# Attention with routed experts on one core: shorter blanks behind each expert's tokens, spaced scatters of one group, ranking of the experts ahead of the head's outputs

## The chip, the cores and the metric

One core of one Trainium2 chip runs the kernel. The metric is the device time of an execution in microseconds (us). Three executions of the kernel before took 619.24 to 621.92 us, with a median of 619.53 us.

## The reference

Attention over 8 batches, 8 heads, 576 positions and 64 features, with a causal window of 128 and a linear bias by distance; the heads side by side give 4608 tokens of 512 features. Each token then goes to one of 8 experts, and the expert's output is scaled by the probability of the choice.

```python
rel = pos[:, None] - pos[None, :]
scores = np.where((rel >= 0) & (rel < 128), q @ k.T / 8 - slope[h] * np.abs(rel), -1e9)
x = (softmax(scores) @ v)                     # then (8 * 576, 8 * 64)
logits = (x / |x|) @ (emb / |emb|).T / tau
expert_idx = np.argmax(logits, axis=1)
probs = softmax(logits)
for e in range(8):
    mask = expert_idx == e
    h = np.maximum(x[mask] @ w1[e], 0.0)      # 512 -> 1024
    out[mask] = gate_w[mask, None] * (h @ w2[e])   # 1024 -> 512
```

With the inputs used, the eight experts receive 611, 541, 517, 513, 507, 670, 573 and 676 tokens.

## The kernel before, in words

Attention works on 36 tiles of 128 tokens, each in two halves. All of it is cut into jobs with an engine, an estimated length, predecessors and a due time; the class `Plan` runs through them once on the host and so fixes the order of instructions on every engine. A job marked `fill` runs where an engine would be free otherwise. A predecessor can carry an extra delay in ns, which moves only the plan's times; `ORDER` (-1e9) in that place asks for order alone. On the chip, engines wait on semaphores for the data and never on the planned times.

Finished tiles are normalised (L718, L724), split into two f16 halves in `rows_buf` (L737 on ACT, L750 on POOL), transposed by a DMA (L754) and multiplied with the expert embeddings on PE (L762, tile `board`). Tiles are routed in groups, `GROUPS = [8, 8, 8, 6, 4, 2]`: a chain of small instructions on DVE and PE finds each token's expert and its place among the expert's tokens, and `put` then scatters a tile's 128 rows to the expert's rows in the DRAM tensor `xs` (L862, indirect DMA on POOL; 36 in all, named `put0` to `put35`). If two puts are neighbours on POOL, a small memset (L861) stands between them. Group 3 holds tiles 24 to 29. In the plan, the puts of groups 0 to 2 have due times 6.4 us apart, those of later groups 1.2 us.

After three groups the fullest expert so far is known, and its first 384 rows, the "head", are computed inside attention as filling work on PE (L937 to L961): `head_y` scales the outputs (L968 on ACT, L970 on DVE) and `head_put` writes them out (L973, L395, POOL). After the last group, DVE ranks the experts by their counts (L378 to L388, eleven small instructions), which gives `ebi` and `nki`, the number of the s-th expert and its count.

The second part, `moe`, goes over the experts by rank in the order `TURNS = [0, 1, 4, 3, 5, 6, 2, 7]`; rank s is computed at a fixed size `SLOTS = [672, 688, 624, 576, 544, 528, 528, 512]`, whatever its count (for rank 0 without the 384 rows of the head). A second plan orders these jobs. For each expert SyncE (SP) does in turn: `blank_rows` (L1251 to L1264), which writes zero rows from the tile `zrow` behind the expert's tokens, so that rows past the count hold no garbage; `rows` (L1266), which reads the expert's rows transposed into `xT` (L1273) and their token numbers and weights (`info`, L1278 and L1285); and `fetch` (L1319, L1321), which loads the weights in f32 into a ring of five buffers `ws`. ACT and DVE split the weights into f16 halves (`w1h` and `w2h`, L1339 and L1347; `w1l` and `w2l`, L1337 and L1350). PE multiplies: `hidden` (L1506), or `product` by a scheme with fewer products (L1455, whose results `e` on ACT and `u` on DVE combine), and `output` (L1555). L1568 and L1570 scale, and POOL scatters to the output (L395). The reading of `rows` waits until the blank and all scatters have landed; a blank need not wait for scatters, which write other rows.

The blank before is one DMA per expert of a fixed number of rows: 288 for rank 0 and 704, 640, 576, 544, 544, 544 and 512 for ranks 1 to 7, of 514 words each. It starts at the expert's count, so it always reaches past the slot's end.

Of the kernel before, what the change touches and what calls it, by code (L numbers as in the profile page):

```python
# [23 lines left out]
P = 128  # L24
# [8 lines left out]
ROW = 514  # L33
SLOTS = [672, 688, 624, 576, 544, 528, 528, 512]
# [14 lines left out]
ORDER = -1e9  # L49
# [12 lines left out]
EXPERT = 9000  # L62
DUE = {'av': -80.7, 'exp': -3.6, 'flip': -24.6, 'gap': 6.4, 'k': -18.2, 'load': -6.9, 'loadv': -2.3, 'logit': -8.2, 'mask': 6.9, 'max': 2.6, 'merge': 1.6, 'norm': 10.8, 'phi': -14.6, 'place': 36.6, 'plo': 1.7, 'put': 18.0, 'q': -14.3, 'route': -1.9, 'score': -29.7, 'v': 3.1, 'xdma': 9.2, 'xhi': 13.9, 'xlo': 16.9, 'xnorm': 24.9}
LAST = 3
MASK = [1230, 1650]
PUT_LANDS, HEAD_LANDS = 4200, 2400

# [98 lines left out]
def kernel(  # L166
# [11 lines left out]
    nc = tc.nc  # L178
# [40 lines left out]
    xs = dram.tile([E, SEG, ROW], F32, name="xs")  # L219
# [33 lines left out]
    zrow = const.tile([P, ROW], F32, name="zrow")  # L253
# [63 lines left out]
    scatters = []  # L317
# [84 lines left out]
    def attention(actx):  # L402
# [6 lines left out]
        stg = actx.enter_context(tc.tile_pool(name="stg", bufs=STG))  # L409
# [555 lines left out]
        def head_y(a):  # L965
            hd["y", a] = y = stg.tile([P, DM], F32, tag="stg", name=f"y_head_{a}")
            if a % 2:
                nc.scalar.activation(y, hd["ps2", a], AF.Copy, scale=hd["gs"][:, a : a + 1])  # L968
            else:
                nc.vector.tensor_scalar(y, hd["ps2", a], hd["gs"][:, a : a + 1], None, op0=ALU.mult)  # L970
# [6 lines left out]
        J = plan.job  # L977
# [155 lines left out]
        def of(gi, what, i):  # L1133
            def f():
                if gi not in box:
                    box[gi] = route_ops(gi)
                x = box[gi][what]
                return x(i) if what == 3 else x() if what == 4 else x[i][2]()

            return f  # L1140

        for gi, G in enumerate(groups):
            T0 = sum(groups[:gi])
            u = 2 * (T0 + G) - 1
            tail = gi == len(groups) - 1
            kinds = [[(e, ns) for e, ns, _ in of_kinds(gi)[w]] for w in (1, 2, 6)]
            prev = [f"xnorm{T}" for T in range(T0, T0 + G)]
            for i, (e, ns) in enumerate(kinds[2]):
                J(f"norm{gi}_{i}", e, ns, of(gi, 5, i), after=prev, due=due("route", u) + 150 * i, uses=[("gn", gi)])
                prev = [f"norm{gi}_{i}"]  # L1150
            scaled = prev[0]
            prev = [f"logit{T0 + G - 1}", "expert_rows", "tables"]
            for i, (e, ns) in enumerate(kinds[0]):
                J(
                    f"route{gi}_{i}", e, ns, of(gi, 1, i), after=prev + ([f"total{gi - 1}"] if i == R_RANK and gi else []), due=due("route", u) + 150 * i,
                    makes=[("rkb", ("rkb", gi))] if i == R_RANK else [], uses=[("rkb", gi)] * (i >= R_RANK),
                )
                prev = [f"route{gi}_{i}"]
                if i == R_RANK - 1:
                    J(f"total{gi}", "DVE", 0 if tail else 270, of(gi, 4, 0), after=prev, due=due("route", u) + 5000)  # L1160
            done = prev[0]
            prev = [f"route{gi}_2", scaled]
            rows_ = [("gx", T) for T in range(T0, T0 + G)]
            for i, (e, ns) in enumerate(kinds[1]):
                J(f"gate{gi}_{i}", e, ns, of(gi, 2, i), after=prev, due=due("route", u) + 150 * (i + 8), uses=rows_ if i in (0, 5) else [])
                prev = [f"gate{gi}_{i}"] if i else prev
            if tail:
                before = [f"route{gi}_{R_RANK}"]
                for i in range(4):
                    J(f"count{i}", "DVE", 90, lambda i=i: count_ops(box[gi][0])[i][2](), after=before, due=due("route", u) + 150 * (i + 10))  # L1170
                    before = [f"count{i}"]
                for i, (e, ns, f) in enumerate(rank_ops({})):
                    J(f"order{i}", e, ns, f, after=before, due=due("route", u) + 150 * (i + 30))
                    before = [f"order{i}"]
            for g in range(G):
                J(
                    f"put{T0 + g}", "POOL", 1180 if gi < LAST else 1270, of(gi, 3, g), dma=750, after=[done, prev[0], f"gate{gi}_0", f"xlo{T0 + g}"], uses=[("gx", T0 + g)],
                    due=due("put", u) + (1000 * DUE["gap"] if gi < LAST else 1200) * g,
                )
            if gi == GP:  # L1180
                ops = [(e, ns) for e, ns, _ in head_ops({})][1:]
                prev = [f"route{gi}_{R_RANK + 1}", "expert_rows"]
                for i, (e, ns) in enumerate(ops):
                    J(f"head{i}", e, ns, (lambda i=i: head_ops(box[GP][0])[1 + i][2]()), after=prev, due=due("route", u) + 150 * (i + 18))
                    prev = [f"head{i}"]
                started = prev[0]
# [21 lines left out]
        for a in range(HEAD // P):  # L1208
            for c in range(6):
                dep = [f"hlo{ft}" for ft in range(FT)] + [f"wlo{2 * KT + i}" for i in range(FT)] if c == 0 else [f"out{a}_{c - 1}"]  # L1210
                J(
                    f"out{a}_{c}", "PE", 4 * 216, lambda b=(a, c): head_output(*b), after=dep + ([f"out{a - 1}_5"] if a and c == 0 else []),
                    makes=[(RING["sc"], ("ps2", a))] if c == 0 else [], uses=[("ps2", a)], due=2e7 + 1000 * a, fill=True,
                )
            J(f"y{a}", "ACT" if a % 2 else "DVE", 600, lambda a=a: head_y(a), after=[f"out{a}_5", "head_info"] + [f"fetch{i}" for i in range(NP)], makes=[("stg", ("y", a))], uses=[("ps2", a)], due=2e7)
            J(f"yput{a}", "POOL", 1200, lambda a=a: head_put(a), after=[f"y{a}"], uses=[("y", a)], due=3e7)
        handed["free"], end = plan.run(dict(FREE))
        handed["rows"] = max(end[f"put{T}"] for T in range(NT)) + LAT["SP"]
# [8 lines left out]
    def moe(mctx):  # L1227
# [25 lines left out]
        def blank_rows(s):  # L1253
            (nb, hb), b0 = blocks(s), first_row(s) // P
            e = state[s]["e"]
            nt = sel_["n0i"][0:1, 0:1] if s == 0 else nki[0:1, s : s + 1]
            n = nc.sync.value_load(nt, min_val=0, max_val=NTOK)
            m = (nb - b0) * P + hb
            d = nc.sync.dma_start(
                xs[ds(e, 1), ds(n, m), :].rearrange("o (a p) c -> p (o a) c", p=32),  # L1260
                zrow[0:32].unsqueeze(1).to_broadcast([32, m // 32, ROW]),
            )
            for p_ in scatters:
                tc.declare_no_dep(d.ins, p_.ins, reason="rows beyond the expert's tokens")  # L1264

        def rows(s):  # L1266
            cap, r0, (nb, hb) = SLOTS[s], first_row(s), blocks(s)
# [688 lines left out]
```

## Time and profile before

| | before |
|---|---|
| median of 3 runs | 619.53 us |
| the profiled execution | 615.1 us |
| its span, first to last instruction | 612.9 us |
| mean granted TensorE clock | 0.974 |
| PE busy | 565.2 us (92%) |
| DVE busy | 476.7 us (78%) |
| ACT busy | 372.0 us (61%) |
| POOL busy | 330.0 us (54%) |

All times in the text are from the profiled execution, counted in us from the start of its span; 2.2 us of that execution lie outside the span. A granted clock of 1.00 is 2.4 GHz on PE and 0.50 is 1.2 GHz. Attention fills the span to about 254 us, where the head's last output ends; the experts follow.

### The profile page before, as it was taken

How to read it: one execution, taken by the hardware profiler on the slowest of the kernel's cores; microseconds unless marked ns; L12 is line 12 of the kernel's file. 1: busy time of each engine (PE TensorE's matmuls, PEld its weight loads, DVE VectorE, ACT ScalarE, POOL GpSimd, SP SyncE). 2: the span in 40 equal slices, each digit the busy share in tenths (PEclk: the TensorE clock that was granted, in tenths of full speed). 3: DMA queues.
4: the chain of work that ended last, by engine and by line, in shares of the span. 5: the costliest groups of instructions: out<-in, count | busy, mean ns of one | idle time of the engine just before them, and what ended most of it. 6: DMA issues, size and time to landing. Idle time of an engine off the chain costs nothing. (4 is left out here: it accounts for less than half of the span.)

```text
span 612.9 us, 16467 instructions
## 1 busy us (share of the span) xinstructions
PE 565.2 (92%) x6097; PEld 369.5 (60%) x6097; DVE 476.7 (78%) x1573; ACT 372.0 (61%) x858; POOL 330.0 (54%) x435
## 2 busy tenths in 40 slices
PE   7999889799978699798999899999899999999996
PEld 3767667666656466363654574574674854754854
DVE  5988988989989676235598796699699799898570
ACT  4999999999999682134462443653653645734320
POOL 7888699899889865302355711442515334433001
PEclk9999999999988989888999999999999999999999
DMA  8699979999999944899978437528658354412001
GB/s 262 162 226 228 242 197 193 255 211 237 232 278 254 200 118 107 213 234 298 269 183 229 190 106 177 185 70 183 249 136 235 127 155 156 136 64 87 14 18 53
DMA packets 121298, 109.88 MB, mean 179 GB/s; under 512 B 85109, under 2 KB 86133, under 8 KB 121216
## 3 DMA queue, kind: packets, MB, share of 16 engines
q1 hardware_dynamic: 115376, 89.89, 59.7%
q0 software_dynamic: 5840, 18.92, 8.2%
q8 instruction: 49, 0.80, 0.5%
q14 instruction: 33, 0.27, 0.1%
HBM read 61.92 MB, written 28.12 MB: 147 GB/s over the span
## 5 line engine op out<-in xcount | busy, mean ns | idle before, releaser
L395 POOL DMA_INDIRECT out_dram<-y,ids x32 | 42.8, 1338 | 132.3 <-ACT y L1568 100.2
L599 ACT ACTIVATE pe<-sb,nm 128x128 f32<-128x128 f32 x288 | 94.8, 390 | 12.2 <-DVE nm L591 11.9
L1555 PE MATMUL ps<-w2h,hh 128*128 128x512 f16 (+1 forms) x264 | 98.4, 373 | 0.0
L1555 PE MATMUL ps<-w2l,hh 128*128 128x512 f16 (+1 forms) x264 | 98.4, 373 | 0.0
L1555 PE MATMUL ps<-w2h,hl 128*128 128x512 f16 (+1 forms) x264 | 98.4, 373 | 0.0
L1555 PEld LDWEIGHTS <-hh 128*128 128x128 f16 x528 | 51.5, 98 | 58.0 <-issue 0.8
L608 PE MATMUL ptp<-ident,pe 128*128 128x128 f32 x288 | 57.8, 302 | 16.5 <-ACT pe L599 6.0
L564 PE MATMUL sc<-k,q 64*64 64x192 f32 (+1 forms) x1152 | 62.4, 333 | 0.0
L512 ACT ACTIVATE pq<-ptp 128x512 f16<-128x512 f32 x78 | 57.5, 737 | 7.7 <-PE ptp L608 6.4
L1568 ACT ACTIVATE y<-ps,gs 128x512 f32<-128x512 f32 (+1 forms) x28 | 19.0, 678 | 70.0 <-PE ps L1555 56.3
L515 DVE SCALAR_TENSOR_TENSOR pq<-ptp,pq 128x512 f16<-128x512 f32 x66 | 49.1, 744 | 9.4 <-ACT pq L512 7.7
L591 DVE CUSTOM_DVE_ANT_0 sb<-sc,tab_full 128x128 f32<-128x128 f32 x224 | 54.7, 279 | 0.0
L608 PEld LDWEIGHTS ptp<-ident,pe 128*128 128x128 f32 x288 | 34.0, 144 | 33.0 <-ACT pe L599 17.9
L1506 PE MATMUL ps<-xT,w1h 128*128 128x288 f16 (+2 forms) x192 | 43.7, 322 | 5.7 <-DMA xT<-xs 3.9
L750 POOL TENSOR_TENSOR rows_buf<-xf,rows_buf 128x512 f16<-128x512 f32 x36 | 43.9, 1221 | 5.3 <-ACT rows_buf L737 5.0
L1337 DVE SCALAR_TENSOR_TENSOR w2l<-ws,w2h 128x1024 f16<-128x1024 f32 x28 | 33.6, 1219 | 16.1 <-ACT w2h L1339 16.1
L1350 DVE SCALAR_TENSOR_TENSOR w1l<-ws,w1h 128x512 f16<-128x512 f32 (+1 forms) x36 | 37.5, 1050 | 9.2 <-ACT w1h L1347 9.2
L1455 PEld LDWEIGHTS <-w1h 128*128 128x128 f16 x384 | 37.6, 98 | 11.6 <-issue 2.7
L564 PEld LDWEIGHTS sc<-k,q 64*64 64x64 f32 x1152 | 37.3, 137 | 11.3 <-issue 5.2
L1555 PEld LDWEIGHTS <-hl 128*128 128x128 f16 x264 | 25.8, 98 | 29.5
L862 POOL DMA_INDIRECT xs<-rows_buf,di x36 | 36.1, 1003 | 12.5 <-issue 4.1
L694 PE MATMUL av<-vh,mp 128*128 128x65 f16 x384 | 39.2, 196 | 3.5 <-POOL mp L646 3.3
(257 smaller groups left out, 1661.2 us busy)
## 6 DMA issues: line engine op xcount, KB each, us to landing
ws<-moe_w_dram SPq DMA_DIRECT2D x56, 512.0 KB
q<-q_dram SPq DMA_DIRECT2D x36, 256.0 KB
ldv<-v_dram SPq DMA_DIRECT2D x36, 256.0 KB
k<-k_dram SPq DMA_DIRECT2D x32, 256.0 KB
stg<-moe_w_dram SPq DMA_DIRECT2D x16, 256.0 KB
xs<-zrow SPq DMA_DIRECT2D x3, 1092.2 KB
xs<-zrow SPq DMA_DIRECT2D x1, 1413.5 KB
xs<-zrow SPq DMA_DIRECT2D x1, 1285.0 KB
```

The costliest lines, as they stand in the source:

```text
L395: ins = nc.gpsimd.indirect_dma_start(out[:, :], bass.IndirectOffsetOnAxis(ap=ids, axis=0), y, None, bounds_check=NTOK - 1, oob_is_err=False)
L512: nc.scalar.activation(hi, ps, AF.Copy, scale=scale)
L515: nc.vector.scalar_tensor_tensor(lo, ps, scale, hi, op0=ALU.mult, op1=ALU.subtract)
L564: nc.tensor.matmul(sc[T, hf, j][l * REM : (l + 1) * REM, i, c0 : c0 + (n1 - n0) * REM].rearrange("p (n c) -> p n c", c=REM), qT[T][rows, h ...
L591: nc.vector.tensor_tensor_reduce(sb_t[T, hf][:, 2 * j + i, :], sc[T, hf, j][:, i, c0 : c0 + P], tab, -QS, BIG, ALU.add, ALU.min, nm_t[T, h ...
L599: nc.scalar.activation(pr_t[T, hf][:, n, :], sb_t[T, hf][:, n, :], AF.Exp, bias=nm_t[T, hf][:, n : n + 1], scale=-1.0)
L608: nc.tensor.matmul(pt.rearrange("p (l j) c -> p l j c", j=2)[:, :, j, i * REM : (i + 1) * REM], pe[:, n, :], ident.rearrange("p (l c) -> p ...
L694: nc.tensor.matmul(o_, a_, b_, start=False, stop=(n == last), skip_group_check=True)
L750: nc.gpsimd.tensor_tensor(xx[:, DM : 2 * DM], xf_t[T], xx[:, 0:DM], op=ALU.subtract)
L1455: nc.tensor.matmul(pq[key], a, b, start=(first and i == 0), stop=(i == len(jobs) - 1), skip_group_check=True)
L1506: nc.tensor.matmul(ps[:, :w], a[:, kt, fs], xx[:, b + kt, c0 : c0 + w], start=(n == 0), stop=(n == len(jobs) - 1))
L1555: nc.tensor.matmul(ps, x[:, ft, a * P : (a + 1) * P], w[:, ft, c], start=(which != 2 and n == 0), stop=(which != 1 and n == len(jobs) - 1) ...
```

## The change

Three edits. First, `blank_rows` issues two DMAs: one of 128 rows, and one for the rest of the old length with a condition, `n + 128 < SLOTS[s]`, n being the expert's count read into a register (for rank 0 its count past the head). With the counts above, n + 128 is at least the slot's size for every rank: 670 + 128 against 672 is the first, 507 + 128 against 512 the last. Second, each scatter of group 3 but its first gets the scatter before it as a predecessor with an extra 2600 ns. Third, the head's `y` jobs come after the last job of the ranking (`order10`) in order.

```diff
 LAST = 3
+SPREAD = 2600
...
                 J(
-                    f"put{T0 + g}", "POOL", 1180 if gi < LAST else 1270, of(gi, 3, g), dma=750, after=[done, prev[0], f"gate{gi}_0", f"xlo{T0 + g}"], uses=[("gx", T0 + g)],
+                    f"put{T0 + g}", "POOL", 1180 if gi < LAST else 1270, of(gi, 3, g), dma=750, after=[done, prev[0], f"gate{gi}_0", f"xlo{T0 + g}"] + ([(f"put{T0 + g - 1}", SPREAD)] if gi == LAST and g else []), uses=[("gx", T0 + g)],
...
-            J(f"y{a}", "ACT" if a % 2 else "DVE", 600, lambda a=a: head_y(a), after=[f"out{a}_5", "head_info"] + [f"fetch{i}" for i in range(NP)], makes=[("stg", ("y", a))], uses=[("ps2", a)], due=2e7)
+            J(f"y{a}", "ACT" if a % 2 else "DVE", 600, lambda a=a: head_y(a), after=[f"out{a}_5", "head_info", ("order10", ORDER)] + [f"fetch{i}" for i in range(NP)], makes=[("stg", ("y", a))], uses=[("ps2", a)], due=2e7)
...
             m = (nb - b0) * P + hb
-            d = nc.sync.dma_start(
-                xs[ds(e, 1), ds(n, m), :].rearrange("o (a p) c -> p (o a) c", p=32),
-                zrow[0:32].unsqueeze(1).to_broadcast([32, m // 32, ROW]),
+            dl = [nc.sync.dma_start(xs[ds(e, 1), ds(n, P), :].rearrange("o p c -> (o p) c"), zrow)]
+            dl.append(
+                nc.sync.dma_start(
+                    xs[ds(e, 1), ds(n + P, m - P), :].rearrange("o (a p) c -> p (o a) c", p=32),
+                    zrow[0:32].unsqueeze(1).to_broadcast([32, (m - P) // 32, ROW]),
+                    cond=(n + P < SLOTS[s]), cond_hint=False,
+                )
             )
-            for p_ in scatters:
-                tc.declare_no_dep(d.ins, p_.ins, reason="rows beyond the expert's tokens")
+            for d in dl:
+                for p_ in scatters:
+                    tc.declare_no_dep(d.ins, p_.ins, reason="rows beyond the expert's tokens")
```

The new lines shift the numbers: L862 is L863 afterwards, L1259 becomes L1260 and L1262, L1273 becomes L1279.

On POOL, around group 3's scatters, the order before (the L646 rows are the masks of attention, which PE waits for; L750 is the low half of a tile):

```order
L646 AFFINE_SELECT mp_33_1_5553<-pq_33_1_5495 128x512
L862 DMA xs_66<-rows_buf_200,di_3_5565 42496x514
L861 MEMSET spare_201 128x1
L862 DMA xs_66<-rows_buf_200,di_3_5565 42496x514
L861 MEMSET spare_201 128x1
...
L862 DMA xs_66<-rows_buf_200,di_3_5565 42496x514
L646 AFFINE_SELECT md_34_0_5763<-pq_34_0_5585 128x512
L646 AFFINE_SELECT mp_34_0_5762<-pq_34_0_5585 128x512
```

and with the change:

```order
L647 AFFINE_SELECT mp_33_1_5553<-pq_33_1_5495 128x512
L863 DMA xs_66<-rows_buf_200,di_3_5565 42496x514
L647 AFFINE_SELECT md_34_0_5637<-pq_34_0_5585 128x512
L647 AFFINE_SELECT mp_34_0_5636<-pq_34_0_5585 128x512
L751 TENSOR_TENSOR rows_buf_200<-xf_32_5443,rows_buf_200 128x512
L863 DMA xs_66<-rows_buf_200,di_3_5565 42496x514
L535 TENSOR_TENSOR vo_35_5756<-ldv_35_5375,vh_193 128x512
L647 AFFINE_SELECT md_34_1_5782<-pq_34_1_5666 128x512
...
L863 DMA xs_66<-rows_buf_200,di_3_5565 42496x514
L862 MEMSET spare_201 128x1
L863 DMA xs_66<-rows_buf_200,di_3_5565 42496x514
L751 TENSOR_TENSOR rows_buf_200<-xf_35_5946,rows_buf_200 128x512
```

Six scatters in a row become four that have three to five other instructions behind each of them, and a pair at the end, ahead of the last tile's low half. The six scatters of groups 4 and 5 stay in one row.

On SP, the blank of the second expert (rank 1) with what each instruction waits for, before (in brackets stand the semaphores, of which DMAHW0 to 7 count landings of SP's DMAs in turn):

```order
L1257 TENSOR_LOAD nki [waits DVE_49]
L1257 ISA x2
L1259 ISA
L1259 DMA xs<-zrow 32x22x514 [waits DMAHW4_49,DMAHW5_49,DMAHW3_49,DMAHW2_49]
L1321 ISA
L1321 DMA ws_1_0_6438<-moe_w_dram 128x2x512 [waits DMAHW6_49]
```

and with the change:

```order
L1258 TENSOR_LOAD nki [waits DVE_49]
L1258 ISA x2
L1260 ISA
L1260 DMA xs<-zrow 128x514 [waits DMAHW5_49,DMAHW6_49,DMAHW4_49,DMAHW3_49]
L1262 ISA x2
L1262 DMA xs<-zrow 32x18x514 [waits DMAHW7_49,DMAHW6_49]
L1327 ISA
L1327 DMA ws_1_0_6436<-moe_w_dram 128x2x512
```

The conditional DMA waits for two landings, DMAHW6 being that of the 128 rows just issued; the weights stand behind it on SP. Each of the eight blanks has this form.

On DVE, the ranking before (its eleven instructions in order, the first two ahead of the head's output):

```order
L378 SCALAR_TENSOR_TENSOR key<-cnt,desc_e 128x8
L379 SCALAR_TENSOR_TENSOR key<-ho,key 128x8
L970 TENSOR_SCALAR y_head_6235<-ps_head_6148,gs_head 128x512
L380 TENSOR_TENSOR gtm<-key 128x64
L375 TENSOR_REDUCE rank<-gtm 128x8
```

and with the change:

```order
L379 SCALAR_TENSOR_TENSOR key<-cnt,desc_e 128x8
L380 SCALAR_TENSOR_TENSOR key<-ho,key 128x8
L381 TENSOR_TENSOR gtm<-key 128x64
...
L389 CAST nki<-nk 128x8
L971 TENSOR_SCALAR y_head_6258<-ps_head_6141,gs_head 128x512
```

All eleven now stand ahead of it. The rest of DVE's, PE's and ACT's order in `moe` is the same, but for a few head jobs and scalings that changed places with a neighbour.

## Rows read from the trace of the kernel before

**Rows 1.** PE's waits by line and releaser, 250 to 612 us (total, times, longest)
```profile
PE ps L1506 <- DMA xT<-xs: 3.9, 1, 3.9
PE pq_b L1455 <- DVE u L1473: 2.0, 1, 2.0
PE ps L1506 <- ACT w1h L1339: 1.9, 1, 1.9
PE pq_a L1455 <- ACT e L1466: 1.6, 1, 1.6
PE ps L1506 <- DVE w1l L1337: 0.8, 1, 0.8
```
**Rows 2.** Windows: us, busy us (instructions) of PE, PEld, DVE, ACT, POOL, then granted clock, DMA share, GB/s
```profile
212.90:219.70 6.80, 4.61 (x26) 2.35 (x26) 3.23 (x16) 4.08 (x12) 2.54 (x5) 0.50 0.60 158
225.00:240.00 15.00, 15.00 (x187) 10.09 (x185) 12.50 (x41) 6.77 (x17) 8.75 (x13) 1.00 0.48 84
257.30:264.10 6.80, 5.71 (x24) 3.52 (x25) 1.68 (x2) 0.83 (x2) 0.79 (x4) 0.50 0.74 168
288.00:291.40 3.40, 3.40 (x12) 1.79 (x13) 1.66 (x2) 1.14 (x2) 0.79 (x1) 0.50 1.06 301
349.50:352.90 3.40, 3.40 (x17) 2.27 (x15) 3.40 (x4) 1.26 (x2) 3.40 (x7) 0.50 0.27 108
```
**Rows 3.** POOL's timeline, 205 to 240 us (start, us, instruction, idle before and its releaser)
```profile
207.06 1.02 POOL L862 DMA_INDIRECT xs<-rows_buf,di  x1 [0.16 <-POOL mp L646]
...
213.43 0.96 POOL L862 DMA_INDIRECT xs<-rows_buf,di  x1 [0.19 <-issue]
214.41 0.65 POOL L646 TENSOR_SCALAR_AFFINE_SELECT md<-pq 128x512 f32<-128x512 f32 x1
...
235.01 1.16 POOL L750 TENSOR_TENSOR rows_buf<-xf,rows_buf 128x512 f16<-128x512 f32 x1 [2.71 <-ACT rows_buf L737]
```
**Rows 4.** PE's timeline, 207 to 217 us
```profile
210.77 0.43 PE L762 MATMUL board<-enc,xT 128*128 128x8 f16 x11 [1.04 <-DMA xT<-rows_buf]
...
212.85 0.33 PE L608 MATMUL ptp<-ident,pe 128*128 128x128 f32 x1 [1.09 <-issue]
215.38 0.77 PE L608 MATMUL ptp<-ident,pe 128*128 128x128 f32 x2 [2.19 <-issue]
```
**Rows 5.** DVE's timeline, 247 to 251 us: the head's first output, the ranking behind it
```profile
248.17 0.75 DVE L970 TENSOR_SCALAR y_head<-ps_head,gs_head 128x512 f32<-128x512 f32 x1 [3.77 <-remote]
...
250.25 0.17 DVE L388 CAST nki<-nk 128x8 int32<-128x8 f32 x1
```
**Rows 6.** SP's timeline, 244 to 330 us (issues: start, us)
```profile
245.27 0.13 SPq L1259 DMA_DIRECT2D xs<-zrow  x1
...
252.86 3.45 SPq L1273 DMA_TRANSPOSE xT<-xs  x1
...
259.50 0.36 SPq L1259 DMA_DIRECT2D xs<-zrow  x1
...
260.66 2.17 SPq L1319 DMA_DIRECT2D ws<-moe_w_dram  x1
268.97 6.36 SPq L1273 DMA_TRANSPOSE xT<-xs  x1
...
324.46 0.38 SPq L1259 DMA_DIRECT2D xs<-zrow  x1
```
**Rows 7.** SP's waits, 244 to 612 us (columns as in rows 1)
```profile
SPq L1273 <- DMA xs<-rows_buf,di: 0.3, 1, 0.3
```
**Rows 8.** Windows while the second expert's blank moves, and just after it (columns as above)
```profile
260.40:267.70 7.30, 7.30 (x47) 5.10 (x46) 1.37 (x3) 1.64 (x4) 0.00 (x0) 0.74 0.96 198
267.80:271.00 3.20, 3.20 (x29) 2.56 (x27) 0.82 (x2) 0.77 (x2) 0.00 (x0) 1.00 0.99 330
```
**Rows 9.** ACT's timeline near 334 us
```profile
333.61 1.06 ACT L1339 ACTIVATE w2h<-ws 128x1024 f16<-128x1024 f32 x1 [6.33 <-DMA ws<-moe_w_dram]
```
**Rows 10.** Window around PE's wait for `u` (columns as above)
```profile
345.00:360.00 15.00, 12.83 (x94) 9.80 (x93) 15.00 (x28) 6.77 (x17) 7.74 (x10) 0.89 0.26 88
```

## The prediction

> **What bounds the kernel now.** PE is busy 92% of the span, so what counts is where it isn't. I read PE's waits first [rows 1]: behind attention PE waits 3.9 us for the first expert's rows at the handoff, 1.9 and 0.8 us for weights of the second expert (ACT's `w1h`, DVE's `w1l`), 2.0 us for DVE's `u` and 1.6 us for ACT's `e`. Then the windows in which the granted clock was half [rows 2]: each comes right behind a stretch in which PE sat idle. 6.8 us at 0.50 lie around 213 to 220 and 257 to 264 us, 3.4 us behind 288 and 349.5 us. A stretch at half the clock with PE busy gives back half of its length when it goes: 1.7 us for one of 3.4. So a wait on PE costs more than itself, and less of it can give back more.
>
> Inside attention I then read 205 to 217 us. POOL issues six scatters in a row from 207.06, the last at 213.43 us [rows 3], about 1.27 us apart, and only then the masks that attention needs, at 214.41. In the same stretch PE is idle for 1.04, 1.09 and 2.19 us [rows 4]; the last two are called issue, waits for nothing that the profile shows, and end right behind the scatters. From 225 to 240 us PE is busy 15.00 of 15 us [rows 2], so time won ahead of that is passed on.
>
> **Scatters of group 3.** With three to five other instructions behind each of the first four scatters, masks come ahead of the second scatter and not behind the sixth. At most all idle time goes: 1.04 + 1.09 + 2.19 = 4.3 us, and the half clock, under which PE was busy 4.61 us [rows 2], gives back 2.3: 6.6 us. At least nothing goes, if the scatters stall PE wherever they stand. The 1.04 us ends with a transposing DMA, which the change does not touch; I leave it. Of the other 3.28 + 2.3 = 5.6 us I leave a fifth to the pair of scatters that still stands together: **-4.5 us** (0 to -6.6). The pair now stands ahead of the last tile's `L750`, ahead of which POOL had 2.71 us idle [rows 3]: two scatters at 1.27 us are 2.5 us and just fit. If they don't, the last group's routing is late, and with it the handoff.
>
> **Ranking and the first blank.** Before, DVE's first head output waited 3.77 us until 248.17 with the ranking behind it, which ended at 250.42 [rows 5]. Now the instructions behind it (1.5 us by those rows) run in that gap, from 244.40, and end near 246. SP needs `ebi` for the weights ahead of the first rows, which it issued at 252.86 [rows 6], after a wait for the last scatter of only 0.3 us [rows 7]: ranking, blank and scatters ended almost together, so all must move. The ranking moves by some 4 us. The blank issued at 245.27 shrinks from 288 to 128 rows of 2056 bytes, 329 kB less; at 198 GB/s [rows 8] that is 1.66 us, by which the scatters' packets behind it come earlier. Against that SP now waits for the 128 rows to land, which I work out below as 3.5 us: 248.8, with the ranking done and before the scatters end. The handoff shrinks by **-1.6 us** (0 to -1.6 of idle; up to -3.3 if the half clock behind it shortens by one step of 3.4 us too, which I don't count, since an idle 2.19 us went with a 6.8 us stretch).
>
> **The second blank.** It was issued at 259.50 and the rows behind it at 268.97 [rows 6]: 9.47 us. Of these 7.3 us moved 704 x 2056 = 1447 kB at 198 GB/s with the DMA engines 0.96 busy [rows 8]; 2.17 us are start and landing. 128 rows are 263 kB: 1.33 + 2.17 = 3.5 us. The conditional DMA is not sent, but SP stands at it until 263.0. Behind it stand two weight loads; before, they were issued by 262.83 (260.66 + 2.17) [rows 6], within 3.0 us after the blank's 0.36. If they take 3.0 us again, rows go out at 266.0, 3.0 us earlier, and so does every load behind them. That covers the 1.85 + 0.79 = 2.64 us on `w1h` and `w1l` [rows 1], and with the idle time the half clock behind it goes: **-4.3 us** (0, if another load is late by as much, to -4.3). Late next would be DVE's `w1l`, with 0.4 us to spare.
>
> The Trainium skill speaks against this edit: "DMA: Bandwidth & Descriptors", section "Rules for kernel authors", advises joining small transfers into one large one, and its section "Anatomy of one DMA — SWDGE (gpsimd) path" fits a DMA as 2.0 us plus bytes over 436 GB/s. By that fit the old blank is an estimated 5.3 us and 128 rows 2.6 us, so the 2.6 us for which SP is now held would eat the 2.7 us won: this term about 0 and the sum -7. The 9.47 us of this trace disagree; the measurement decides.
>
> **The blank at 324.46** [rows 6] moved 544 rows; 416 fewer are 4.3 us at 198 GB/s, less about 2.2 us for the landing that the loads behind it now wait for: 2.1 us. ACT's `w2h` at 333.61 had waited 6.33 us for a load [rows 9], and two steps on stands PE's wait of 2.0 us for `u`. But DVE is then busy 15.00 of 15 us [rows 10], so part of that is its own work. I take half the wait and leave the clock: **-1.0 us** (0 to -2.0 - 1.7 = -3.7).
>
> **The other five blanks**, and 16 more SP instructions: 0. No wait in rows 1 ends with what stands behind them; the 1.6 us on `e` is ACT's own. If that cover is gone, each can cost up to the 2.2 us of a landing.
>
> **Sum:** -4.5 - 1.6 - 4.3 - 1.0 = -11.4 us. Against the profiled 615.1 us that is 603.7; the median of the runs shown is 4.4 us higher, 619.53, which gives **608 us**.
>
> **Rivals.**
> 1. *The scatters stall PE wherever they stand*, or the stall passes to the pair and the six behind it. For it: groups 4 and 5 keep their row of six, and PE's late signals had no releaser that I can name. Against it: POOL's masks stand behind the burst. Only the blanks gain: -6.9, 612.6 us.
> 2. *The blanks' bytes were hidden.* Weights and DVE set the pace behind the handoff: for it, DVE's 15.00 of 15 [rows 10]; against it, PE waits for what loads feed [rows 1, 9]. Left are -4.5 and -1.6: 613.4 us.
> 3. *The condition does not spare the bytes.* The second DMA runs for all rows, or its wait lasts as long. Then each blank takes its old time and a landing more: the handoff and both weight waits grow by about 2.2 us at two places, the scatters still gain 4.5: about 619 us. Against it: n + 128 reaches the slot's size for all eight counts.
> 4. *SP's hold costs more than the bytes* (slower). Loads are issued 3.0 us later at the second blank and at that of 324.46, and the first blank is held 3.5 us for 1.66 us of bytes: +1.8 + 3.0 + 3.0 = +7.8 if PE waits for loads by their issue and not by bytes, less 4.5: +3.3, 622.8 us. It decides where DMA engines had room beside the blank, so that a load issued early also landed early. Against it: 0.96 busy at 198 GB/s, and 330 GB/s only after it [rows 8]. The same page of the Trainium skill, section "Rules for kernel authors", advises to issue a DMA early and wait on its semaphore late; here SP does the opposite, and no trace of before shows what that costs.
> 5. *Everything goes in full:* -6.6 - 3.3 - 4.3 - 3.7 = -17.9, 601.6 us.
>
> **How the numbers follow.** About 0.5%, 3.1 us, is what a measurement of this kernel can tell from no change, so faster is below 616.4. Forecast 0.47; rival 1 0.17; 2 0.16; 3 0.08; 4 0.06; 5 0.06. The forecast, 5 and nearly all of 1 and 2 are faster: 0.82. Rival 3 and the weak ends of 1 and 2 are the same: 0.13; slower 0.05. The range takes in the forecast with its terms' bounds, 1, 2 and most of 5: 602 to 616; the outer ends of 3 and 4 are left out.
>
> **What would show it.** In the profile after: masks between the scatters, and no `issue` wait of 1 us or more on PE near 213 to 216; no 6.8 us at half the clock there. DVE's ranking before its first head output. Blank DMAs of 257 KB (eight, and no others), 3.5 us from issue to the load behind. The handoff's wait at 2.3 us instead of 3.9; no wait for `w1h` or `w1l` at the second expert, and no half clock there; the wait for `u` near 1. The prediction is wrong if PE's idle time near the scatters comes back within 20 us; if new waits for weights of over 1 us stand behind any blank; or if the whole moves by less than 3 us.

## The result and the profile after

The changed kernel takes 611.41 us (median of 4 runs, 609.36 to 612.68) against 619.47 us of the kernel before on the same chip: a ratio of 0.9865, 95% interval 0.9829 to 0.9901, so 8.1 us faster, where 11.4 had been worked out. The profiled execution took 609.36 us with a span of 607.6 us, 5.3 us less than that of before.

Where these 5.3 us come from needs care, since the two executions differ already where the programs don't: the first scatter of group 3 starts at 207.06 us before [rows 3] and at 211.56 us after, and PE's order is the same up to 3.7 us past that scatter (before) and 2.6 us past it (after). The head's outputs end at 254.51 us before and at 255.43 after, so up to there the changed kernel's execution is no shorter. From that scatter on the changed kernel gains 9.8 us: 3.6 up to the end of the head's outputs, -1.1 at the handoff, 7.3 from the first expert's first product to the last.

PE's waits from 250 us on, after (line, releaser; total us, times, longest), against [rows 1]:

```profile
PE ps L1512 <- DMA xT<-xs: 5.0, 1, 5.0
PE pq_b L1461 <- DVE u L1479: 3.2, 2, 1.7
```

The waits for `w1h`, `w1l` and `e` are gone, the one for `u` has become two, and the wait for the first rows has grown from 3.9 to 5.0 us. Two windows of the same trace (columns as in [rows 2]) show the clock: half for most of the 6.8 us behind the handoff, as before, and whole where it had been half behind the second expert's weights:

```profile
260.40:267.20 6.80, 6.80 (x33) 4.35 (x34) 0.86 (x2) 0.82 (x2) 1.85 (x5) 0.57 0.43 150
...
280.00:292.00 12.00, 12.00 (x71) 6.80 (x70) 7.69 (x9) 6.70 (x10) 3.09 (x4) 1.00 0.72 262
```

POOL's timeline after, around the first two scatters of group 3 (start, us, instruction): masks and a tile's low half stand between them, as the order said.

```profile
211.56 1.02 POOL L863 DMA_INDIRECT xs<-rows_buf,di  x1 [0.16 <-POOL mp L647]
212.60 0.64 POOL L647 TENSOR_SCALAR_AFFINE_SELECT md<-pq 128x512 f32<-128x512 f32 x1
213.19 0.64 POOL L647 TENSOR_SCALAR_AFFINE_SELECT mp<-pq 128x512 f32<-128x512 f32 x1
213.79 1.17 POOL L751 TENSOR_TENSOR rows_buf<-xf,rows_buf 128x512 f16<-128x512 f32 x1
215.12 1.25 POOL L863 DMA_INDIRECT xs<-rows_buf,di  x1 [0.17 <-issue]
```

PE has one idle stretch of 1 us or more there, a wait that has a releaser, and 1.4 us behind its end the clock is half for 3.4 us (a window with columns as in [rows 2]), where before it was half for 6.8:

```profile
217.11 0.46 PE L763 MATMUL board<-enc,xT 128*128 128x8 f16 x12 [1.74 <-DMA xT<-rows_buf]
...
218.50:221.90 3.40, 3.40 (x12) 1.57 (x11) 3.24 (x10) 2.69 (x7) 1.75 (x3) 0.50 0.25 87
```

DVE after, 246 to 251 us, answers to [rows 5]: the ranking ends at 246.35, 3.6 us ahead of the head's first output.

```profile
246.18 0.17 DVE L389 CAST nki<-nk 128x8 int32<-128x8 f32 x1
249.91 0.75 DVE L971 TENSOR_SCALAR y_head<-ps_head,gs_head 128x512 f32<-128x512 f32 x1 [3.56 <-remote]
```

SP's issues after, against [rows 6]. L1260 is the blank of 128 rows; L1262 is the conditional DMA, which stands in the trace but moves nothing: the execution's DMAs moved 103.04 MB, and 109.88 before, 6.84 less, which is what the rows past the first 128 come to (3328 rows of 2056 bytes). The `n` of the condition is the expert's whole count for rank 0 too, and not, as the section on the change has it, its count past the head: with 384 fewer, n + 128 would lie below 672 and the second DMA would go out.

```profile
245.58 0.22 SPq L1260 DMA_DIRECT2D xs<-zrow  x1
248.77 0.09 SPq L1262 DMA_DIRECT2D xs<-zrow  x1
250.43 0.36 SPq L1325 DMA_DIRECT2D ws<-moe_w_dram  x1
251.73 3.87 SPq L1279 DMA_TRANSPOSE xT<-xs  x1
...
260.81 0.38 SPq L1260 DMA_DIRECT2D xs<-zrow  x1
263.72 0.08 SPq L1262 DMA_DIRECT2D xs<-zrow  x1
263.99 0.41 SPq L1327 DMA_DIRECT2D ws<-moe_w_dram  x1
264.60 0.34 SPq L1325 DMA_DIRECT2D ws<-moe_w_dram  x1
265.14 8.32 SPq L1279 DMA_TRANSPOSE xT<-xs  x1
```

Two things are to be seen. The second blank holds SP for 2.9 us (260.81 to 263.72) and rows go out 4.3 us behind it, 9.5 before. And the first expert's rows were asked for 3.7 us ahead of the head's end (255.43), 1.6 us ahead before, yet PE got them later: 8.7 us after their issue, 5.5 before.

### The profile page after: what moved, and what is told of

Its sections match the earlier page's. It is cut to its first block, busy times and chain, and to the rows that moved or that the text cites. A ratio compares the mean times of both kernels' runs of the same rounds, so it can differ in the third digit from the quotient of the medians.

```text
span 607.6 us, 16502 instructions
## 1 busy us (share of the span) xinstructions
PE 562.4 (93%) x6097; PEld 370.5 (61%) x6097; DVE 483.1 (80%) x1573; ACT 373.6 (61%) x858; POOL 339.6 (56%) x431
## 2 busy tenths in 40 slices
DMA packets 117970, 103.04 MB, mean 170 GB/s; under 512 B 85109, under 2 KB 86133, under 8 KB 117888
## 5 line engine op out<-in xcount | busy, mean ns | idle before, releaser
L396 POOL DMA_INDIRECT out_dram<-y,ids x32 | 51.3, 1602 | 126.3 <-ACT y L1574 86.9
L1512 PE MATMUL ps<-xT,w1h 128*128 128x288 f16 (+2 forms) x192 | 42.4, 315 | 5.0 <-DMA xT<-xs 5.0
L1356 DVE SCALAR_TENSOR_TENSOR w1l<-ws,w1h 128x512 f16<-128x512 f32 (+1 forms) x36 | 40.2, 1127 | 6.4 <-ACT w1h L1353 5.2
L863 POOL DMA_INDIRECT xs<-rows_buf,di x36 | 37.2, 1034 | 14.0 <-DVE rn L836 4.8
L695 PE MATMUL av<-vh,mp 128*128 128x65 f16 x384 | 41.2, 200 | 3.4 <-POOL mp L647 3.0
L565 PEld LDWEIGHTS sc<-k,q 64*64 64x64 f32 x1152 | 37.2, 137 | 11.4 <-issue 5.2
L647 POOL TENSOR_SCALAR_AFFINE_SELECT md<-pq 128x512 f32<-128x512 f32 x48 | 31.2, 650 | 18.8 <-DVE pq L516 8.3
```

Of the source, the lines that this page charges most:

```text
L396: ins = nc.gpsimd.indirect_dma_start(out[:, :], bass.IndirectOffsetOnAxis(ap=ids, axis=0), y, None, bounds_check=NTOK - 1, oob_is_err=False)
L565: nc.tensor.matmul(sc[T, hf, j][l * REM : (l + 1) * REM, i, c0 : c0 + (n1 - n0) * REM].rearrange("p (n c) -> p n c", c=REM), qT[T][rows, h ...
L695: nc.tensor.matmul(o_, a_, b_, start=False, stop=(n == last), skip_group_check=True)
L1356: nc.vector.scalar_tensor_tensor(dst, src, scale, hi, op0=ALU.mult, op1=ALU.subtract)
L1512: nc.tensor.matmul(ps[:, :w], a[:, kt, fs], xx[:, b + kt, c0 : c0 + w], start=(n == 0), stop=(n == len(jobs) - 1))
```

## Experiments

The kernel before took between 611.5 and 624.3 us on the chips that the runs fell on, so only ratios to it on the same chip are compared. For the parts of an execution, this table has four stretches of each profiled execution, from the timelines: from the first scatter of group 3 to the end of the head's outputs, PE's wait at the handoff, and from the first expert's first product to the last product of all; then the time in which the 2304 packets of 256 bytes of the first rows' transposing read moved, with the number of packets of the head's outputs (4096 bytes each) that started in it. Each row is one execution.

```
kernel           scatter-head end   handoff   first-last product   read's packets (head's in it)
before                 47.45          3.88         349.12              2.82 (12)
after                  43.87          4.98         341.81              5.46 (97)
spread_alone           44.41          5.97         347.70              3.39 (31)
blank_alone            43.39          4.86         342.22              5.70 (61)
order_alone            44.67          4.10         349.74              2.61 (7)
no_order               43.34          4.92         341.38              6.20 (64)
no_second              43.35          2.07         336.59              2.62 (0)
no_second_again        43.37          1.88         337.70              2.77 (0)
always_second          44.12          3.63         358.49              2.74 (25)
no_headput             43.85          3.28         341.02              3.29 (0)
late_put               44.10          2.68         344.78              3.18 (0)
after_again            43.37          2.57         339.87              3.85 (57)
swap                   43.86          2.87         338.12              2.62 (0)
blank_swap             42.62          1.92         338.62              2.84 (0)
```

### Each part alone, and the change without its third part

Four runs on one chip (before: 613.88 us). The first is the kernel before with the second edit alone (the line is shown from `after=` on):

```diff
-after=[done, prev[0], f"gate{gi}_0", f"xlo{T0 + g}"]
+after=[done, prev[0], f"gate{gi}_0", f"xlo{T0 + g}"] + ([(f"put{T0 + g - 1}", SPREAD)] if gi == LAST and g else [])
```

> The kernel before with the spaced scatters alone. Theory (the parts act on their own, each in its place): PE's two waits called issue near 213 and 215 us (1.09 and 2.19 us) and the half clock behind them go, the head's outputs end about 3.5 us earlier against the scatters' group, and the waits for weights (1.9 and 0.8 us), u (2.0) and e (1.6) stay: 3.0 to 4.5 us faster, ratio 0.993 to 0.995. Rival (the stall moves to another place inside attention or to the handoff): PE's idle time near the scatters goes and the handoff's wait of 3.9 us grows to 6 or more, under 1.5 us faster.

Measured: ratio 1.0015, interval 0.9981 to 1.0049. No gain; the forecast's first term isn't there. The handoff's wait is 6.0 us, and the waits behind it stay, much as before:

```profile
PE ps L1507 <- DMA xT<-xs: 6.0, 1, 6.0
PE pq_b L1456 <- DVE u L1474: 2.5, 2, 1.7
PE ps L1507 <- ACT w1h L1340: 2.3, 1, 2.3
PE pq_a L1456 <- ACT e L1467: 1.4, 1, 1.4
...
```

The rival that the stall moves to the handoff would fit this run by its numbers, but the next two show something else. What made the handoff's wait 6.0 us in this one execution is not shown.

The first edit alone, the kernel before with the new `blank_rows`:

```diff
-            d = nc.sync.dma_start(
-                xs[ds(e, 1), ds(n, m), :].rearrange("o (a p) c -> p (o a) c", p=32),
...
+            dl = [nc.sync.dma_start(xs[ds(e, 1), ds(n, P), :].rearrange("o p c -> (o p) c"), zrow)]
...
+                    cond=(n + P < SLOTS[s]), cond_hint=False,
```

> The kernel before with the shorter blanks alone. Theory: the burst of scatters stalls PE as before (idle 1.0, 1.1 and 2.2 us, half clock behind it); the waits for the second expert's weights (2.6 us and 1.7 us of clock) go, the one for u shrinks by about 0.7, the one for e (1.6 us) goes: 5 to 7 us faster, ratio 0.989 to 0.992, and the handoff's wait is about 2.5 us. Rival (the handoff's longer wait in the changed kernel is the price of the shorter first blank, under which the loads and the head's outputs run together): handoff 4.5 us or more, 4 to 5 us faster.

Measured: ratio 0.9873, 0.9833 to 0.9914: the whole gain of the change, 8 us, which is more than the theory (5 to 7) or its rival (4 to 5) had. The waits for `w1h`, `w1l` and `e` are gone as in the changed kernel, the one for `u` did not shrink (two of 3.7 us together), and the handoff's wait is 4.9 us, the rival's number. In this kernel POOL issues the six scatters in a row as before:

```profile
208.96 1.01 POOL L862 DMA_INDIRECT xs<-rows_buf,di  x1 [0.16 <-POOL mp L646]
...
215.72 0.96 POOL L862 DMA_INDIRECT xs<-rows_buf,di  x1 [0.19 <-issue]
```

and PE's longest idle stretch in 206 to 240 us is this one:

```profile
214.68 0.46 PE L762 MATMUL board<-enc,xT 128*128 128x8 f16 x12 [0.80 <-DMA xT<-rows_buf]
```

So the same burst, with the masks behind it, stalled nothing here. PE's and ACT's instructions stand in the very order of before in this kernel, in the one of the third edit alone that follows and in the last one of all (`blank_swap`), and none of these three has a wait called issue there in its waits by line and releaser.

The third edit alone, in the `y` jobs of the kernel before:

```diff
-after=[f"out{a}_5", "head_info"]
+after=[f"out{a}_5", "head_info", ("order10", ORDER)]
```

> The kernel before with the ranking ahead of the head's outputs alone. Theory: the ranking ends near 246 instead of 250.4 us, but the rows of the first expert still wait for the last scatters and the blank, so nothing moves: within 1 us, ratio 0.999 to 1.001. Rival (the ranking is what holds up the handoff): handoff 1 to 2 us shorter, ratio 0.997 or less.

Measured: 0.9979, 0.9943 to 1.0015: nothing that can be told from no change, as expected. It also has the burst unchanged, and neither wait called issue; its first column is 44.67 us, against 47.45 in the profiled execution of before.

The changed kernel without the third edit (the same two lines the other way round):

> The changed kernel without its third part (ranking behind the first head output as before). Theory A: the part does nothing by itself, the time is that of the changed kernel (ratio to before 0.985 to 0.988). Theory B (the earlier ranking lets SP load and read earlier, beside the head's outputs that POOL writes, and the transposing read of 5.4 us became one of 8.6): handoff's wait back at 3.9 us or less and 1 us or more faster than the changed kernel. Rival (the ranking is needed early as soon as blanks are short): handoff 6 us or more and 1 to 2 us slower than the changed kernel.

Measured: 0.9854, 0.9810 to 0.9898, the changed kernel's ratio: theory A. The handoff's wait stays at 4.9 us, so the earlier ranking isn't what prolongs it, and theory B falls as far as it blamed the ranking. This kernel differs from the one with the first edit alone only in the spaced scatters, and on the same chip the two take 605.35 and 605.63 us: the spacing does nothing with short blanks either.

### Bytes or hold

The next runs were made on another chip (before: 622.64 us). In the changed kernel, the second DMA of each blank is taken out:

```diff
-            dl.append(
-                nc.sync.dma_start(
...
-                    cond=(n + P < SLOTS[s]), cond_hint=False,
-                )
-            )
```

> The changed kernel without the conditional DMA (left out: the rows past the first 128, which no expert here asks for). It takes SP's wait for the landing of the 128 rows away. Theory (the hold is covered: SP would stand at the rows' reading anyway): within 1 us of the changed kernel, ratio to before 0.985 to 0.989. Rival (each hold of 2.8 to 7 us on SP delays weights): 2 us or more faster than the changed kernel, the waits for u near 345 and 350 us (1.7 and 1.6) gone.

Measured: 0.9693, 0.9645 to 0.9742. PE's waits from 250 us on:

```profile
PE ps L1505 <- DMA xT<-xs: 2.1, 1, 2.1
PE pq_b L1454 <- DVE u L1472: 1.0, 1, 1.0
```

Once more on a third chip (before: 624.34 us):

> The run without the conditional DMA (left out: the rows past the first 128, which no expert here asks for) once more, on another chip if it so falls, since the kernel before took 622.6 us on the chip of the first and 611.5 on that of the run with the two DMAs swapped. Theory (SP's hold costs some 8 us, as the first of these runs said by its ratio of 0.9693): ratio 0.965 to 0.975 again. Rival (that ratio is one chip's, on which the kernel before was slow; the hold costs 2 us or less, as the swapped DMAs said): ratio 0.980 to 0.988.

Measured: 0.9611, 0.9548 to 0.9673. By these ratios the hold on SP would cost 10 us or more, but the kernel before is some 10 us slower on these two chips than on those of the runs above and below, the changed kernel was not run on them, and the swapped DMAs below say otherwise. The second profile also has a wait for `u` of 1.7 us again, which the first had lost:

```profile
PE pq_b L1454 <- DVE u L1472: 2.1, 2, 1.7
```

The opposite: the condition always holds, so all bytes move again:

```diff
-                    cond=(n + P < SLOTS[s]), cond_hint=False,
+                    cond=(n < NTOK), cond_hint=True,
```

> The changed kernel with a condition that always holds: every blank again writes all its rows, in two DMAs, and SP waits for the first. Theory (the gain behind the handoff is that of the bytes): the second expert's waits for weights (1.9 and 0.8 us) and the 1.6 us on e come back and 1 to 4 us more for the hold and the second landing: 0 to 4 us slower than before, ratio 1.000 to 1.006. Rival (the split itself helps, by freeing or ordering something on SP): still 4 us or more faster than before.

Measured: 1.0046, 1.0006 to 1.0086. All the gain is gone. The waits that the change removed are back and longer, the one for `e` (1.6 us in [rows 1]) among them:

```profile
PE ps L1512 <- DMA xT<-xs: 3.6, 1, 3.6
PE pq_b L1461 <- ACT xSh L1431: 3.2, 1, 3.2
PE pq_b L1461 <- DVE u L1479: 3.1, 2, 2.0
PE pq_a L1461 <- ACT e L1472: 2.9, 1, 2.9
PE ps L1512 <- ACT w1h L1345: 2.4, 2, 1.6
PE ps L1512 <- DVE w1l L1343: 1.6, 2, 0.8
```

Since splitting the blanks without dropping bytes gains nothing, the gain is that of the rows that are no longer written. How much of it is due to their being written from 32 partitions, at 159 to 221 GB/s a blank in the trace of before where the changed kernel's from 128 reach 323, is open: full-length blanks from 128 partitions were not run.

### The handoff

The head's outputs and the first rows' read meet in the changed kernel. POOL issued the first two of these outputs here, on both sides of the read's issue at 251.73:

```profile
250.94 1.00 POOL L396 DMA_INDIRECT out_dram<-y_head,ids_head  x1 [2.08 <-DVE y_head L971]
...
252.24 1.00 POOL L396 DMA_INDIRECT out_dram<-y_head,ids_head  x1 [0.19 <-issue]
```

Windows over the read's packets, before and then after (columns as in [rows 2]): DMA engines are about as busy (a mean share of 1.23 and 1.11), and move 237 and 181 GB/s.

```profile
254.95:257.77 2.82, 0.00 (x0) 0.00 (x0) 0.36 (x2) 1.06 (x1) 0.98 (x1) 0.92 1.23 237
```

```profile
254.06:259.51 5.45, 1.37 (x7) 0.40 (x5) 1.89 (x2) 1.06 (x1) 0.00 (x0) 0.99 1.11 181
```

A run without these writes, and then one that delays them:

```diff
         def head_put(a):
             nc.gpsimd.memset(spare, 0.0)
-            put_rows(hd["ids"][:, a : a + 1], hd["y", a])
```

> The changed kernel without the three DMAs that write the head's outputs (left out: the output rows of the head's 384 tokens). Theory (the first rows' transposing read, whose packets took 5.4 us instead of 2.8, is slowed by the head's outputs, which now move at the same time): its packets back at 2.6 to 3.0 us, the handoff's wait 2.5 us or less instead of 5.0, 2 to 4 us faster than the changed kernel. Rival (it is slow because it runs while PE still works on the head, or because of the blank): packets 5 us or more and the handoff's wait 4.5 us or more.

Measured: 0.9734, 0.9677 to 0.9790, on a chip on which the changed kernel was not run, so that only the traces can be compared. The read's packets take 3.3 us, near the 2.6 to 3.0 expected. But the handoff's wait is 3.3 us, because something else ends it:

```profile
254.13 0.66 PE L1511 MATMUL ps<-xT,w1h 128*128 128x288 f16 x2 [3.28 <-DVE y_head L971]
```

DVE scaled the head's last output only at 253.33, behind the first `w1l` of the next weights (252.19, 1.23 us), ahead of which it stands in the order of before. So a second limit lies close behind the first. The run that delays the writes has, in `rows`:

```diff
+            if s == TURNS[0]:
+                for p_ in head_puts:
+                    sync_dep(p_, dl[0])
```

> The changed kernel with the head's outputs written only when the first expert's rows have landed. Theory (as for the run without these writes): handoff's wait 2.5 us or less, 2 to 4 us faster than the changed kernel, unless the second expert's blank and loads, which now meet these writes, lose it again. Rival (the writes are not what slows the read): handoff's wait 4.5 us or more, no gain.

Measured: 0.9804, 0.9761 to 0.9848, on the chip of the first run without the second DMA. The read's packets take 3.2 us, the handoff's wait is 2.7 us, again ended by `y_head`. But now the writes, at 258.20 and later, meet the second expert's read, which SP takes 12.10 us to issue (8.32 in the changed kernel), and the waits for its weights are back:

```profile
PE ps L1516 <- DVE y_head L971: 2.7, 1, 2.7
PE ps L1516 <- ACT w1h L1349: 2.4, 1, 2.4
PE pq_b L1465 <- DVE u L1483: 0.9, 1, 0.9
PE ps L1516 <- DVE w1l L1347: 0.8, 1, 0.8
```

That the two kinds of transfer slow each other is shown, in single executions of two kernels that change only these writes; without them the read is quick although PE still works on the head in its first 1.6 us. Delaying the writes moves the loss, from the handoff to the second expert (2.68 + 344.78 = 347.5 us against 4.98 + 341.81 = 346.8; 342.4 in the repeat below).

### The other order of the two DMAs

Three runs on one chip (before: 611.53 us): the changed kernel again, the same with the conditional DMA first, and that form of the blanks alone in the kernel before.

```diff
-            dl = [nc.sync.dma_start(xs[ds(e, 1), ds(n, P), :].rearrange("o p c -> (o p) c"), zrow)]
-            dl.append(
+            dl = [
                 nc.sync.dma_start(
...
                     cond=(n + P < SLOTS[s]), cond_hint=False,
                 )
-            )
+            ]
+            dl.append(nc.sync.dma_start(xs[ds(e, 1), ds(n, P), :].rearrange("o p c -> (o p) c"), zrow))
```

> The changed kernel once more, on the chip of the two runs that follow: ratio to before 0.982 to 0.990.

Measured: 0.9868, 0.9805 to 0.9931, as at first. Its six times fall into 600.49 to 601.30 us and 607.17 to 607.93. The profiled execution is one of the first kind: its handoff's wait is 2.6 us, ended by `y_head`, and the read's packets take 3.9 us. By the table it is 2.4 us ahead of the first profile at the handoff and 1.9 us ahead behind it, some 1.2 of these by a half clock of 3.4 us instead of 6.8.

> The changed kernel with the two DMAs of each blank in the other order: the conditional one first, then the 128 rows. It computes the same; what SP waits for ahead of the second is now the end of a DMA that is not sent. Theory (the hold on SP costs some 8 us, as the run without the conditional DMA says): 1 to 2% faster than the changed kernel, ratio to before 0.966 to 0.975, handoff's wait near 2 us, no 1.7 us on u near 345. Rival (a skipped DMA is told as ended only when the queue ahead of it has landed, so SP is held by another wait): no gain over the changed kernel.

Measured: 0.9860, 0.9810 to 0.9910, 602.50 us against 601.01 of the changed kernel: no difference. The skipped DMA lets SP go at once (256.61, then 257.05):

```profile
256.61 0.10 SPq L1261 DMA_DIRECT2D xs<-zrow  x1
257.05 0.36 SPq L1267 DMA_DIRECT2D xs<-zrow  x1
257.61 0.41 SPq L1327 DMA_DIRECT2D ws<-moe_w_dram  x1
258.21 0.35 SPq L1325 DMA_DIRECT2D ws<-moe_w_dram  x1
260.22 8.61 SPq L1279 DMA_TRANSPOSE xT<-xs  x1
```

so the rival that SP is held by another wait falls too. But rows still go out 3.6 us after the first of the two DMAs (260.22), 4.1 to 4.3 with the hold, and the waits for `u` shrink from some 3 us to 0.9:

```profile
PE pq_b L1461 <- DVE u L1479: 0.9, 1, 0.9
```

In the traces that is 338.1 against 339.9 and 341.8 us from first to last product. Some 1.2 us of the larger difference are again the shorter half clock behind the handoff, so at most 1.7 to 2.5 us are left for the hold, which the medians don't show.

> The kernel before with the blanks of the run just above, without spaced scatters and without the moved ranking. Theory (neither of those two does anything): within 0.4% of the run just above. Rival (with short blanks the handoff waits for the ranking or for the scatters): 0.5% or more slower than it, the handoff's wait 4 us or more.

Measured: 0.9803, 0.9755 to 0.9851, 599.93 us, with a handoff's wait of 1.9 us. The point lies below that of the run just above by 0.6%, more than the theory's 0.4% and the other way than its rival has it, and the intervals overlap. Its blanks don't hold SP either, yet the waits for `u` are back at 2.5 us:

```profile
PE pq_b L1460 <- DVE u L1478: 2.5, 2, 1.7
```

With short blanks and the hold, these waits come to 2.8 to 3.7 us in four profiles (changed kernel, its repeat, first edit alone, without the third) and to 0.9 and 2.0 in the two whose writes of the head were altered; without the hold to 0.9, 1.0, 2.1 and 2.5 us. What the hold costs at this place is not settled by that. The kernel has the lowest ratio of those on this chip, and has neither of the two edits inside attention; that it beats the changed kernel (0.9868, interval up to 0.9931 and down to 0.9805) isn't settled.

## Why the prediction was right, and where it was wrong

The time lies in the range, and the direction holds. Of its four terms one was right, one nearly, one was not there, one came out as a loss in one profile and as forecast in the next, and one of the zeros should have been a gain. That the total came so near is in part luck: the -4.5 that were not there were in part made up by the -2.0 that had been put at nothing.

- **Scatters of group 3, -4.5: nothing.** The step that failed is the one that took the idle stretches of 1.09 and 2.19 us [rows 4] for the burst's doing. They were called issue, and they stood in one execution. Three other kernels with the same burst and the same order don't have them, and the spacing alone gives 1.0015. In the profiled pair the 3.6 us are real, but they are what the first profile had too much: 47.45 us in the first column, where all others have 42.6 to 44.7. What made that one execution stall is open.
- **Ranking and first blank, -1.6: +1.1 in the profile, -1.3 in its repeat.** The step held as far as it went: the ranking moved 4.1 us (250.42 to 246.35) and rows went out 2.1 us earlier against the head's end. What failed was to take the read's 5.5 us from issue to use as fixed. Issued earlier it meets the head's outputs, which I hadn't placed in time at all; its packets took 5.5 us instead of 2.8. The ranking did none of it: without that edit the ratio is the same.
- **The second blank, -4.3: -4.7.** Between the first and the second expert's products the offset of the two traces goes from +2.1 to -2.7 us, and both waits and the half clock are gone. The blank held SP 2.9 us, where 3.5 had been worked out, and rows went out 5.1 us sooner behind its issue, not 3.0: its packets come from 128 partitions and took 86 ns each, not the 159 ns of those from 32, and the two weight loads were issued within 1.4 us. The Trainium skill's fit ("DMA: Bandwidth & Descriptors", section "Anatomy of one DMA — SWDGE (gpsimd) path") makes an estimated 2.6 us of these 263 kB, near the 2.9, and 5.3 of the old 1447 kB, where the trace has 9.5; by it the term would have been nothing. The Trainium skill gives that fit for DMAs of GpSimd, and these are SP's. The measurement decides: the old blank moved at 198 GB/s [rows 8].
- **The blank at 324.46, -1.0: -0.7.** Near as a number, and by a sum of two: the first wait for `u` shrank from 2.0 to 1.5 us and lost its half clock, and a second of 1.7 us came behind it and took most of that back. The second is no price of the short blanks: with the long ones it stood in `spread_alone` too (1.7 us at 353.87), behind a first wait of 0.75 us and a whole clock. So what the clock gave back here was waited for `u` again. With all bytes the two waits for `u` come to 3.1 us, without the second DMA to 1.0 and 2.1.
- **The other five blanks, 0: -2.0.** The step "the 1.6 us on `e` is ACT's own" failed. With short blanks the wait is gone, with all bytes it is 2.9 us. ACT worked late there because a load was late behind the blank issued at 419.99, as this row of before's ACT timeline says, which I hadn't read; after, the same instruction waits for no load:

```profile
431.64 1.06 ACT L1339 ACTIVATE w2h<-ws 128x1024 f16<-128x1024 f32 x1 [2.63 <-DMA ws<-moe_w_dram]
```

```profile
425.57 1.05 ACT L1345 ACTIVATE w2h<-ws 128x1024 f16<-128x1024 f32 x1
```

Of the rivals, the first has the right outcome (only the blanks gain, 612.6 us worked out, 611.4 measured), though not its mechanism: no stall moved, there was none to move. The second fell with the blanks alone, which give the whole gain, the third by the bytes counted, and the fifth with the scatters. Of the fourth, SP's hold, a part may be true: at most 1.7 to 2.5 us in the trace of the swapped order, against 2.7 to 7.0 us for which SP stands at each blank. How much of that reaches the time is open, since the ratios of the runs without the second DMA come from chips on which the changed kernel did not run.

## What to carry to other kernels

Idle time that one execution shows without a releaser is no term of a sum until a second execution shows it too; a kernel with the same order around the place serves as well. When a transfer is made to start earlier, list what else moves on the DMA engines in its new place: here the read that left 2 us earlier arrived later. And follow a wait on an engine back to that engine's own waits before calling it the engine's own.

## What the runs showed of the hardware that was not expected

- Seven of the eight blanks of before, which write zero rows from 32 partitions, had a median of 158 to 160 ns per packet of 2056 bytes and moved their rows at 159 to 197 GB/s. From 128 partitions the packets of the changed kernel took 85 to 87 ns, and the blanks moved at up to 323 GB/s. The third of before's blanks (at 286.40 us) had a median of 85 ns too, with weight loads moving beside it, and still moved its own rows at no more than 221 GB/s. A blank of full length from 128 partitions was not tried.
- A transposing read of 2304 packets of 256 bytes took 2.6 to 3.3 us with no packets of the head's indirect writes among them, 2.6 to 3.4 with 7 to 31, and 3.9 to 6.2 us with 57 to 97, though 64 of these need only 0.64 us of 16 engines at the 159 ns that they take elsewhere.
- A conditional DMA that isn't sent takes SP 0.1 us and counts as landed almost at once: the DMA behind it went out 0.4 us later (256.61 and 257.05). What it waits for itself, it waits for all the same.
- The kernel before differs by 2% from chip to chip (611.5 to 624.3 us), and the changed kernel has two groups of times some 6.5 us apart on one chip. Its two profiles differ by 4.3 us from the handoff on, but they come from two chips, and none is of the slower group there, so what parts the groups is open.
